# Weighted sums of the first attention stage, formed with the values as weights

## The chip, the cores and the metric

The kernel runs on one core of a Trainium2 chip. The metric is device time of one execution in microseconds (us). Before the change three runs gave 1503.12, 1503.74 and 1511.39 us; the median is 1503.74.

## What is computed

Two attentions one behind the other (32 packed queries `p` gather from keys and values, then the 576 queries gather from the packed result), then two gated MLPs. Cut from the reference:

```python
batch, n_heads, seq, head_dim, n_pack = 8, 8, 576, 64, 32
def sm_attn(qq, kk, vv):
    s = scale * np.matmul(qq, kk.transpose(0, 1, 3, 2))
    s = s - np.max(s, axis=-1, keepdims=True)
    a = np.exp(s)
    a = a / (np.sum(a, axis=-1, keepdims=True) + 1e-09)
    return np.matmul(a, vv)
p_packed = sm_attn(p, k, v)
out = sm_attn(q, p_packed, p_packed)
# x: out as (4608, 512)
h = x @ w_in;  y = (h * sigmoid(h)) @ w_out
h2 = y @ w_in2;  result = (h2 * cos(h2)) @ w_out2
```

## The kernel before

The program records every operation first and a planner then sets the order. `Plan.add` notes what each operation reads and writes and gives it a cost from a table (`price`, lines 163 to 193); `Plan.schedule` places the operations on the engines by these costs and by due times (`due_first`, line 1186); the instructions are then written out in that order, each engine's in its own queue. Buffers are rings: a ring's next tile is handed out in the order in which the program records, so an operation that writes it waits for the last reader of what it held. An operation recorded inside `plan.either()` may go to ScalarE or VectorE, as the planner finds. Where the planner sees TensorE idle in the first 60 us, it puts in filler matmuls (`busy`, line 1201; 64 columns, result unused). Since all operations are written out by one helper, the profile shows line 213 for nearly everything, and tiles tell them apart.

*First stage* (`stage1`, line 808), once for each batch b and group g of four heads. The keys come turned (`mem.turned`); `scores` multiplies them with the packed queries (tile `pbd`) into two banks of PSUM; the row maximum, the copy to `a1` and the exponential follow, which also sums each row (`sums`); `rs` is the reciprocal of the sum (lines 824 to 826). `a1` holds 128 rows (four heads of 32 packed queries) and 576 columns. It is turned in chunks by TensorE (line 835) and copied to `a1t`: five chunks of 128 columns, the last of 64, in the steady class `Steady`; six of 96 in `Boot`, which serves batches 0 and 1. Then come the weighted sums (lines 840 to 850): the softmax chunk is the weight (32 columns, one head), the values move (64 columns):

```python
for c in range(n):
    for j in range(2):
        for h2 in range(2):
            h = 32 * (2 * j + place(g, h2))
            T.matmul(st[h : h + 32, :D], a1t[: lens[c], c, h : h + 32], vt(c, h2, j), ...)
```

The result is scaled by `rs` into `pp` (line 852), turned once more by TensorE (line 854) and copied to `ppf` (line 856), which is what the second stage and `products` read. In the trace `a1`, `a1t` and `pp` are tiles `big` in the steady class, and `ba`, `bat` and `bpp` in the boot class; the values are `vin`, and `bx` in the boot class.

*Second stage* (`stage2`, line 860): scores of all queries against `ppf`, softmax on VectorE and ScalarE, and the turned result as a pair of rounded parts in `a2` (trace: `a`), a ring of six buffers, two for a batch. *Products* (line 907) multiply `ppf` with the first MLP's input weights, so that the first MLP (`first`, line 955) reads `a2` and these products. It runs in 208 steps of 16 hidden blocks: 64 steps for batches 0 and 1 (`BLOCKS[0]`), then nine blocks of 16 steps over 320 or 512 tokens. The attention of batches 2 to 7 is recorded between these steps by `firsts` (line 1221), `seconds` (line 1228) and the loops from line 1269 on. From about 700 us the second MLP runs.

Of the kernel before, what the change touches and what calls it, by code (L numbers as in the profile page):

```python
# [12 lines left out]
F32 = mybir.dt.float32  # L13
F32R = mybir.dt.float32r
I32 = mybir.dt.int32
U32 = mybir.dt.uint32
AF = mybir.ActivationFunctionType
ALU = mybir.AluOpType
# [417 lines left out]
def attention_mlps_kernel(  # L436
# [13 lines left out]
    B, H, S, D = q.shape  # L450
# [3 lines left out]
    P = 128  # L454
# [12 lines left out]
    plan = Plan(nc)  # L467
# [4 lines left out]
    V, A, T, G, DMA = plan.V, plan.A, plan.T, plan.G, plan.D  # L472
# [7 lines left out]
    def ring(ts):  # L480

        at = cycle(ts)
        return lambda: next(at)
# [5 lines left out]
    bpool = boot_stack.enter_context(pool("boot", "right"))  # L489
# [4 lines left out]
    a2p = mid.enter_context(pool("a2p"))  # L494
    top = mid.enter_context(ExitStack())
    att = top.enter_context(pool("att"))
# [3 lines left out]
    def tiles(pl, shape, dtype, name, n):  # L500

        ts = [pl.tile(shape, dtype, name=f"{name}{i}") for i in range(n)]
        cells.setdefault(pl, []).extend(t.tensor.name for t in ts)
        return ts


    def place(g, h2):
        return (g + h2) % 2
# [39 lines left out]
    ident = const.tile([P, P], F32, name="ident")  # L548
# [10 lines left out]
    def copy(dst, src):  # L559
        with plan.either():  # L560
            A.copy(dst, src)
            V.tensor_copy(dst, src)
# [93 lines left out]
    mx2s = ring(tiles(att, [P, NB], F32, "mxb", 2))  # L656
    rs2s = ring(tiles(att, [P, NB], F32, "rsb", 2))
    ppfs = ring(tiles(att, [P, 2, 2 * NP], F32, "ppf", 4))
    a2s = ring(tiles(a2p, [P, 2, S], F32R, "a2", 6))

    pin = {}

# [19 lines left out]
    def cut(t, shape):  # L682
        t = t[:, : math.prod(shape[1:])]
        return t if len(shape) == 2 else t.rearrange("p (a b) -> p a b", a=shape[1])
# [4 lines left out]
    class Steady:  # L689
# [4 lines left out]

        def __init__(self):
            self.kins = ring(tiles(att, [P, NB, 32], F32, "kin", 2))
            self.vins = ring(tiles(att, [P, 4 * len(self.chunks), D], F32, "vin", 1))
            self.bigs = ring(tiles(att, [P, len(self.chunks) * P], F32, "big", 3))

        def get(self, name, shape, g, j=0):  # L700
            return cut(self.bigs(), shape)

        def turned(self, src, b, g, bank):

# [35 lines left out]
    class Boot:  # L740
# [7 lines left out]
        def __init__(self):  # L748
            self.x = dict(zip("kvq", tiles(bpool, [P, H, NCH, D], F32, "bx", 3)))
            self.kt = tiles(bpool, [P, S], F32, "bkt", 4)  # L750
            self.a = tiles(bpool, [P, S], F32, "ba", 2)
            self.at = tiles(bpool, [P, NCH * P], F32, "bat", 2)
            self.pp = tiles(bpool, [P, P], F32, "bpp", 2)

        def load(self, n, src, b):
            plan.unit = ("load", n, b)
# [8 lines left out]
        def get(self, name, shape, g, j=0):  # L765
            if name == "a1":
                return self.a[g]
            return cut({"kt": self.kt[2 * g + j], "s": self.a[g], "pp": self.pp[g]}.get(name, self.at[g]), shape)

        def turned(self, src, b, g, bank):  # L770
            x = self.x["k" if src is k else "q"]
# [16 lines left out]
    ppf = {}  # L788
    a2 = {}
# [18 lines left out]
    def stage1(b, g, bank, mem):  # L808
        plan.unit = ("stage1", b, g)

        plan.margin = plan.SPARE if b >= 2 else 0
        chunks = mem.chunks
        kt = mem.turned(k, b, g, bank)
        a1 = mem.get("a1", [P, S], g)
        mx = maxes()
        sts = scores(g, pbds[b % 2][:, 2 * g : 2 * g + 2], lambda h2: h2, kt, bank, mem.spot)
        for hf, st in enumerate(sts):
            V.tensor_reduce(mx[:, hf : hf + 1], st, axis=AX.X, op=ALU.max)
            copy(a1[:, hf * HALF : (hf + 1) * HALF], st)
        m = ms()  # L820
        V.tensor_scalar(m, mx[:, 0:1], mx[:, 1:2], -SCALE, op0=ALU.max, op1=ALU.mult)
        sums = sumss()
        A.activation(a1[:, :S], a1[:, :S], AF.Exp, bias=m, scale=SCALE, accum_out=sums)
        rs = rss()
        V.tensor_scalar(rs, sums, 1e-9, None, op0=ALU.add)
        V.reciprocal(rs, rs)
        chunks = mem.chunks
        n = len(chunks)
        lens = [len(range(S)[c]) for c in chunks]
        a1t = mem.get("a1t", [P, n, P], g)  # L830
        for c0, c1 in ((0, 4), (4, n)):
            st = bank()
            r = lens[c0]
            for c in range(c0, c1):
                T.transpose(st[:r, (c - c0) * P : (c - c0 + 1) * P], a1[:, chunks[c]], ident)
            copy(a1t[:r, c0:c1, :], st[:r, : (c1 - c0) * P].rearrange("p (c n) -> p c n", n=P))
        vt = mem.values(b, g)
        st = bank()
        with plan.together():
            for c in range(n):  # L840
                for j in range(2):
                    for h2 in range(2):
                        h = 32 * (2 * j + place(g, h2))
                        T.matmul(
                            st[h : h + 32, :D],
                            a1t[: lens[c], c, h : h + 32],
                            vt(c, h2, j),
                            start=(c == 0),
                            stop=(c == n - 1),
                        )  # L850
        pp = mem.get("pp", [P, 2, D], g)
        V.tensor_scalar(pp, st[:, :D].unsqueeze(1).to_broadcast([P, 2, D]), rs, None, op0=ALU.mult)
        st = bank()
        T.transpose(st[:, :P], pp.rearrange("p h d -> p (h d)"), ident)
        t = ppfs()
        copy(t, st[:, :P].rearrange("p (j n) -> p j n", j=2))
        ppf[b, g] = t
        plan.margin = 0

    def stage2(b, g, bank, mem):  # L860
# [331 lines left out]
    boot = Boot()  # L1192
# [28 lines left out]
    def firsts(b, mem, banks):  # L1221
        if b % 2 == 0:
            load_p(b)
        place_p(b)
        for g in range(2):
            stage1(b, g, banks[g], mem)

    def seconds(b):
        for g in range(2):
            for f in stage2(b, g, bank, steady):  # L1230
                f()
# [7 lines left out]
    boot.load("q", q, 0)  # L1239
    pairs = [ring([acc[g], acc[2 + g]]) for g in range(2)]  # L1240
    for g in range(2):
        stage1(0, g, pairs[g], boot)
    fs = [stage2(0, g, ring([hb[g], pairs[g]()]), boot) for g in range(2)]
    for f in sum(map(list, zip(*fs)), []):
        f()
# [23 lines left out]
    for o in range(BLOCKS[0]):  # L1269
# [3 lines left out]
        x = o - 48  # L1273
        if x >= 0 and x % 4 == 3:
            products(x // 4, (2,))
    firsts(3, steady, [bank, bank])
    for j, s0 in enumerate(BLOCKS[:-1]):
        b = 3 if j == 0 else j // 3 * 2 + j % 3 + 3 if j % 3 else B
        if j == 6:
            plan.release = LATER  # L1280
            for F in range(2):
                for c in range(2):
                    win2_unit(F, c)
                for c in range(4 * F, 4 * F + 4):
                    wout2_unit(c)
                    wout2_unit(c + FH)
            plan.release = 0.0
        for o in range(FC):
            first(s0 + o)
            if b < B:  # L1290
                if o % 4 == 3:
                    products(o // 4, (b,))
                if o == 7:
                    seconds(b)
        if j % 3 < 2 and (n := j // 3 * 2 + j % 3 + 4) < B:
            firsts(n, steady, [bank, bank])

    change(top, [att], "yp", "right", raws + ys, {len(raws) + i: n for i, n in ((1, 32), (2, 32), (3, 32), (4, 32), (5, 64), (6, 64), (7, 64), (8, 64))})
    change(mid, [a2p], "cp", "left", ns + rs_ + g2s + os_)
# [44 lines left out]
```

## Time and profile before

| | us |
|---|---|
| three runs | 1503.12, 1503.74 (median), 1511.39 |
| the profiled execution, its own time | 1507.88 |
| its span, first to last instruction | 1506.1 |
| busy: TensorE | 1492.0 (99%) |
| busy: VectorE | 1147.5 (76%) |
| busy: ScalarE | 756.6 (50%) |
| granted TensorE clock, mean | 0.996 |

The trace belongs to the profiled execution, which took 1.8 us beyond its span. Busy time of TensorE (PE) counts matmuls from issue to modelled end, so neighbours overlap; the distance from one start to the next tells what a matmul costs. PEld is the loading of weights, which overlaps PE. The granted clock is 1.00 for 2.4 GHz and 0.50 for 1.2 GHz.

### The profile page before, as it was taken

The numbers are of one execution on the slowest core, as the hardware profiler recorded it, in microseconds if no ns is written. First come the engines' busy times: TensorE is split into PE (matmuls) and PEld (weight loads), VectorE is DVE, ScalarE is ACT, GpSimd is POOL, SyncE is SP. The second block draws the span as 40 slices with busy tenths as digits, with TensorE's granted clock in tenths as the row PEclk, the third lists the DMA queues.
The fourth block names the chain that finished last, engine by engine and source line by source line (L and its number), as shares of the span: only waits on it lengthen the run. The fifth ranks groups of instructions, "written<-read, shape, count | busy, mean of one in ns | idle before, by whom it ended". The sixth has DMA issues, their size and how long they took to land.

```text
span 1506.1 us, 29441 instructions
## 1 busy us (share of the span) xinstructions
PE 1492.0 (99%) x10790; PEld 1329.8 (88%) x10790; DVE 1147.5 (76%) x2361; ACT 756.6 (50%) x1554; POOL 0.7 (0%) x6
## 2 busy tenths in 40 slices
PE   8999999999999999999999999999999999999998
PEld 6898988878998888989989999899989999999997
DVE  6899877977787967866387778878777777777765
ACT  6776554645455454545454444544444444444443
POOL 0000000000000000000000000000000000000000
PEclk9899999999999999999999999999999999999999
DMA  9676666676767666465776658676666657575550
GB/s 266 197 229 192 171 179 158 166 199 164 201 175 232 165 189 174 144 224 180 263 259 205 203 180 268 203 248 215 218 198 200 203 181 227 177 229 179 186 190 33
DMA packets 313968, 296.23 MB, mean 197 GB/s; under 512 B 172512, under 2 KB 218080, under 8 KB 313824
## 3 DMA queue, kind: packets, MB, share of 16 engines
q1 hardware_dynamic: 313824, 294.35, 64.7%
q8 instruction: 85, 1.39, 0.4%
q14 instruction: 59, 0.48, 0.1%
HBM read 242.81 MB, written 51.45 MB: 195 GB/s over the span
## 4 chain that ended last, share of the span: by engine, by line
PE 92%; DMA 3%; DVE 2%; SPq 1%; ACT 1%; issue 0%; DVEq 0%; ACTq 0%
PE acc L213 51%; PE hb L213 23%; PE mb L213 9%; PE sb L213 9%; DMA ysb<-ypart 2%; SPq L213 1%; DVE r L213 1%; DMA wd<-in_moe_w_in 1%; PE acc L1203 0%; DMA w<-w2s 0%; DMA bx<-in_k 0%; DVE raw L213 0%; ACT bkt L213 0%; DVE wd L213 0%; DMA out<-o 0%
## 5 line engine op out<-in xcount | busy, mean ns | idle before, releaser
L213 PE MATMUL acc<-g,w 128*128 128x320 f32 (+2 forms) x2496 | 469.1, 327 | 0.0
L213 PE MATMUL acc<-w,g 128*128 128x512 f32 x1728 | 432.0, 392 | 0.1
L213 PEld LDWEIGHTS acc<-g,w 128*128 128x128 f32 x2496 | 383.8, 188 | 45.3 <-issue 23.4
L213 PEld LDWEIGHTS acc<-w,g 128*128 128x128 f32 x1728 | 310.6, 189 | 56.3 <-ACT ysb L213 0.5
L213 PE MATMUL hb<-a,w 128*128 128x320 f32 (+2 forms) x1536 | 264.7, 299 | 2.5 <-DVE gf L213 2.2
L213 PEld LDWEIGHTS hb<-a,w 128*128 128x128 f32 x1536 | 227.4, 190 | 22.4 <-issue 8.2
L213 DVE TENSOR_TENSOR g<-gf,g 128x320 fp32r<-128x320 f32 (+2 forms) x208 | 107.8, 521 | 53.5 <-PE acc L213 41.0
L213 ACT ACTIVATE gf<-hb 128x320 f32<-128x320 f32 (+2 forms) x208 | 95.4, 466 | 102.8 <-PE hb L213 89.8
L213 ACT CAST g<-gf 128x320 fp32r<-128x320 f32 (+2 forms) x186 | 90.9, 490 | 103.8 <-PE acc L213 88.0
L213 DVE SCALAR_TENSOR_TENSOR gf<-gf,hb 128x320 f32<-128x320 f32 (+2 forms) x208 | 105.1, 517 | 40.8 <-ACT gf L213 39.8
L213 ACT ACTIVATE r<-r,half_pi 128x512 f32<-128x512 f32 x144 | 103.6, 720 | 36.9 <-DVE r L213 36.6
L213 ACT CAST g<-r 128x512 fp32r<-128x512 f32 x144 | 89.5, 621 | 60.4 <-DVE r L213 58.0
L213 PEld LDWEIGHTS hb<-w,w 128*128 128x128 f32 x744 | 105.5, 190 | 8.0
L213 PE MATMUL hb<-w,w 128*128 128x256 f32 x744 | 111.8, 282 | 0.0
L213 DVE TENSOR_TENSOR g<-r,g 128x512 fp32r<-128x512 f32 x144 | 98.7, 686 | 11.9 <-ACT g L213 11.6
L213 DVE SCALAR_TENSOR_TENSOR r<-n,r 128x512 f32<-128x512 int32 x144 | 99.0, 687 | 2.3
L213 ACT ACTIVATE n<-hb 128x512 int32<-128x512 f32 x72 | 43.1, 598 | 109.7 <-PE hb L213 107.7
L213 DVE TENSOR_TENSOR hb<-hb,gf 128x256 f32<-128x256 f32 x72 | 31.1, 431 | 68.5 <-PE hb L213 68.2
L213 ACT ACTIVATE n<-mb 128x512 int32<-128x512 f32 x36 | 21.5, 598 | 95.0 <-PE mb L213 95.0
L213 PE MATMUL mb<-w,w 128*128 128x256 f32 x456 | 65.8, 283 | 0.0
L213 PE MATMUL sb<-w,w 128*128 128x256 f32 x456 | 65.8, 283 | 0.0
L213 DVE TENSOR_SCALAR r<-r 128x512 f32<-128x512 f32 x144 | 60.8, 423 | 2.6
(206 smaller groups left out, 1897.0 us busy)
## 6 DMA issues: line engine op xcount, KB each, us to landing
w<-w2s SPq DMA_DIRECT2D x504, 256.0 KB, 3.6
w<-w1dram SPq DMA_DIRECT2D x96, 256.0 KB, 4.0
w2s<-wd SPq DMA_DIRECT2D x28, 512.0 KB, 3.9
wd<-in_moe_w_in SPq DMA_DIRECT2D x24, 512.0 KB, 4.8
wd<-in_moe_w_out SPq DMA_DIRECT2D x20, 512.0 KB, 4.2
raw<-ydram SPq DMA_DIRECT2D x72, 128.0 KB, 3.8
w2dram<-wd SPq DMA_DIRECT2D x16, 512.0 KB, 2.9
w<-w2dram SPq DMA_DIRECT2D x16, 512.0 KB, 5.5
```

The source lines that it names most:

```text
L213: run = lambda: emit(*[real(x) for x in args], **{k: real(x) for k, x in kw.items()})
```

## The change

- `a1` is multiplied by `rs` right behind the exponential (576 columns, ScalarE or VectorE); the scaling into `pp` is gone.
- `stage1` ends with the turned chunks; a new function `weighted` forms the sums, for both groups of a batch in one piece and one bank (for batches 0 and 1 group by group). The values are the weights now (64 columns) and the softmax chunk moves (32 columns), so that the result comes out turned: the transpose of `pp` is gone. The chunks are the inner loop under j.
- `ppf` is filled by four copies of 64 rows by 64 elements for each group, where it was one of 128 by 128.
- Buffers: `a2` four in place of six; `vin` two in place of one; the turned chunks get two buffers `a1t` of their own, and the three `bigs` shrink to 576 columns.
- The loops: `firsts(3)` is recorded in step 59 in place of behind step 63; `seconds` always at a block's first step in place of its eighth, and for batches 4 to 7 one block later.

```diff
-    a2s = ring(tiles(a2p, [P, 2, S], F32R, "a2", 6))
+    a2s = ring(tiles(a2p, [P, 2, S], F32R, "a2", 4))
...
-            self.vins = ring(tiles(att, [P, 4 * len(self.chunks), D], F32, "vin", 1))
-            self.bigs = ring(tiles(att, [P, len(self.chunks) * P], F32, "big", 3))
+            self.vins = ring(tiles(att, [P, 4 * len(self.chunks), D], F32, "vin", 2))
+            self.bigs = ring(tiles(att, [P, S], F32, "big", 3))
+            self.a1ts = ring(tiles(att, [P, len(self.chunks) * P], F32, "a1t", 2))
...
-        chunks = mem.chunks
+        with plan.either():
+            V.tensor_scalar(a1[:, :S], a1[:, :S], rs, None, op0=ALU.mult)
+            A.activation(a1[:, :S], a1[:, :S], AF.Copy, scale=rs)
...
-        vt = mem.values(b, g)
+        plan.margin = 0
+        return lens, a1t, mem.values(b, g)
+
+    def weighted(b, parts, bank):
+        plan.unit = ("stage1", b, min(parts))
+
+        plan.margin = plan.SPARE if b >= 2 else 0
         st = bank()
         with plan.together():
-            for c in range(n):
+            for i, (g, (lens, a1t, vt)) in enumerate(parts.items()):
+                n = len(lens)
                 for j in range(2):
-                    for h2 in range(2):
-                        h = 32 * (2 * j + place(g, h2))
-                        T.matmul(
-                            st[h : h + 32, :D],
-                            a1t[: lens[c], c, h : h + 32],
-                            vt(c, h2, j),
-                            start=(c == 0),
-                            stop=(c == n - 1),
-                        )
-        pp = mem.get("pp", [P, 2, D], g)
-        V.tensor_scalar(pp, st[:, :D].unsqueeze(1).to_broadcast([P, 2, D]), rs, None, op0=ALU.mult)
-        st = bank()
-        T.transpose(st[:, :P], pp.rearrange("p h d -> p (h d)"), ident)
-        t = ppfs()
-        copy(t, st[:, :P].rearrange("p (j n) -> p j n", j=2))
-        ppf[b, g] = t
+                    for c in range(n):
+                        for h2 in range(2):
+                            h = 32 * (2 * j + place(g, h2))
+                            T.matmul(
+                                st[64 * h2 : 64 * h2 + 64, D * i + 32 * j : D * i + 32 * j + 32],
+                                vt(c, h2, j),
+                                a1t[: lens[c], c, h : h + 32],
+                                start=(c == 0),
+                                stop=(c == n - 1),
+                            )
+        for i, g in enumerate(parts):
+            t = ppfs()
+            for h2 in range(2):
+                for r in (64 * h2, 64 - 64 * h2):
+                    x = 32 * place(g, h2)
+                    copy(t[r : r + 64, :, x : x + 32], st[64 * h2 : 64 * h2 + 64, D * i : D * i + D].rearrange("p (j n) -> p j n", j=2))
+            ppf[b, g] = t
         plan.margin = 0
...
-        for g in range(2):
-            stage1(b, g, banks[g], mem)
+        parts = {g: stage1(b, g, banks[g], mem) for g in range(2)}
+        if b == 1:
+            for g in range(2):
+                weighted(b, {g: parts[g]}, banks[g])
+        else:
+            weighted(b, parts, banks[0])
...
-    firsts(3, steady, [bank, bank])
+        if o == 59:
+            firsts(3, steady, [bank, bank])
...
-        b = 3 if j == 0 else j // 3 * 2 + j % 3 + 3 if j % 3 else B
+        x = j // 3 * 2 + 2
+        b = (3 if j == 0 else B, x + 2, x + 3)[j % 3]
+        c = (x + 1, B, x + 2)[j % 3]
...
-            if b < B:
-                if o % 4 == 3:
-                    products(o // 4, (b,))
-                if o == 7:
-                    seconds(b)
+            if b < B and o % 4 == 3:
+                products(o // 4, (b,))
+            if c < B and o == 0:
+                seconds(c)
```

**How the order moves.** TensorE, the weighted sum of batch 2's second group, before the change (`acc` and `hb` are the first MLP, `vin` the moving values, `big` the softmax as weights; a call stands for two passes; first the moving operand, then the weights):

```order
L213 MATMUL acc_88<-g_154,w_1098 128x288
L213 MATMUL acc_89<-g_154,w_1098 128x288
L213 MATMUL sb<-vin_176,big_179 32x64 x20
L213 MATMUL acc_90<-g_154,w_1098 128x288
L213 MATMUL acc_91<-g_154,w_1098 128x288
L213 MATMUL hb_93<-a_136,w_1102 128x288 x3
```

and the sums of batch 2 with the change:

```order
L213 MATMUL acc_90<-g_152,w_1108 128x288
L213 MATMUL acc_91<-g_152,w_1108 128x288
L213 MATMUL sb<-a1t_177,vin_172 64x32 x20
L213 MATMUL sb<-a1t_178,vin_173 64x32 x20
L213 MATMUL acc_90<-g_152,w_1108 128x288
L213 MATMUL acc_91<-g_152,w_1108 128x288
L213 MATMUL hb_92<-a_136,w_1111 128x288 x3
```

Both groups stand together; the values have become the weights, the output is 64 rows by 32 columns, and there are 40 calls in one piece where there were 20 twice.

TensorE in the start, the sums of batch 0 (`bat` the softmax, `bx` the values, `bpp` the scaled result, line 1203 and after it line 1213 the fillers, `w1e,ppf` the first products), before:

```order
L213 MATMUL acc_88<-bx_158,bat_166 32x64 x24
L1203 MATMUL acc_89<-ident 128x64 x3
L213 MATMUL acc_90<-ident,bpp_168 128x128
L1203 MATMUL acc_88<-ident 128x64
L213 MATMUL mb<-w1e_146,ppf_132 32x512 x2
L213 MATMUL mb<-w1e_147,ppf_132 32x512 x2
L1203 MATMUL acc_88<-ident 128x64 x14
L213 MATMUL acc_89<-bx_158,bat_167 32x64 x24
```

and with the change:

```order
L213 MATMUL acc_88<-ident,ba_162 96x128 x4
L213 MATMUL acc_90<-ident,ba_162 96x128 x2
L1213 MATMUL acc_89<-ident 128x64 x9
L213 MATMUL acc_89<-ident,ba_163 96x128 x4
L213 MATMUL acc_91<-ident,ba_163 96x128 x2
L213 MATMUL acc_88<-bat_164,bx_156 64x32 x24
L1213 MATMUL acc_89<-ident 128x64 x3
L213 MATMUL mb<-w1e_144,ppf_132 32x512 x2
L213 MATMUL mb<-w1e_145,ppf_132 32x512 x2
L1213 MATMUL acc_88<-ident 128x64 x8
L213 MATMUL acc_89<-bat_165,bx_156 64x32 x24
```

The transpose of `bpp` is gone between sum and product; nine fillers stand ahead of the second group's transposes, and eight in place of fourteen ahead of its sum.

VectorE, the last writing of `a2` for batch 5 with the change (`a_139`; `gf<-gf,hb` is the multiplication of a step of the first MLP, of which 126 stand ahead of it):

```order
L213 SCALAR_TENSOR_TENSOR gf_148<-gf_148,hb_92 128x320
L213 STREAM_TRANSPOSE big_175<-big_174 128x576
L213 SCALAR_TENSOR_TENSOR gf_149<-gf_149,hb_93 128x320
L213 STREAM_TRANSPOSE big_174<-kin_171 128x576
L213 TENSOR_TENSOR a_139<-big_175,a_139 128x576
L213 TENSOR_TENSOR g_151<-gf_148,g_151 128x320
```

Before, the same writing went to a buffer of its own, `a_141`, behind 120 multiplications; it has come six steps nearer to step 128, which reads it.

## Rows read from the trace of the kernel before

**Rows 1.** The page, part 1 (busy us, share, instructions) and part 4 (chain by engine).

```profile
PE 1492.0 (99%) x10790; PEld 1329.8 (88%) x10790; DVE 1147.5 (76%) x2361; ACT 756.6 (50%) x1554; POOL 0.7 (0%) x6
PE 92%; DMA 3%; DVE 2%; SPq 1%; ACT 1%; issue 0%; DVEq 0%; ACTq 0%
```

**Rows 2.** Stretches of the span; the first line names the columns.

```profile
core 0: us, PE busy (x) PEld busy (x) DVE busy (x) ACT busy (x) POOL busy (x), PEclk, DMA share, GB/s
0.00:40.00 40.00, 34.11 (x433) 27.08 (x433) 26.18 (x79) 24.77 (x59) 0.70 (x6) 1.00 1.02 265
40.00:44.00 4.00, 3.83 (x31) 2.21 (x30) 3.56 (x11) 3.38 (x8) 0.00 (x0) 0.64 1.08 251
44.00:48.00 4.00, 4.00 (x19) 4.00 (x20) 3.58 (x9) 3.30 (x9) 0.00 (x0) 0.50 1.06 244
48.00:52.00 4.00, 4.00 (x21) 3.91 (x21) 0.99 (x6) 1.79 (x6) 0.00 (x0) 0.58 1.04 335
52.00:80.00 28.00, 27.14 (x275) 23.80 (x274) 27.43 (x76) 23.68 (x60) 0.00 (x0) 1.00 0.42 141
80.00:700.00 620.00, 618.54 (x4993) 543.47 (x4992) 487.99 (x985) 333.70 (x706) 0.00 (x0) 1.00 0.66 184
700.00:1506.00 806.00, 800.37 (x5030) 725.29 (x5028) 597.76 (x1204) 365.94 (x711) 0.00 (x0) 1.00 0.63 204
```

**Rows 3.** Order of time, TensorE, around batch 2's first weighted sum (start, us, what).

```profile
148.08 1.36 PE L213 MATMUL hb<-a,w 128*128 128x288 f32 x9
149.27 0.56 PE L213 MATMUL acc<-g,w 128*128 128x288 f32 x3
...
156.35 0.82 PE L213 MATMUL acc<-g,w 128*128 128x288 f32 x5
157.10 0.90 PE L213 MATMUL sb<-vin,big 128*32 128x64 f32 x40
157.93 0.40 PE L213 MATMUL acc<-g,w 128*128 128x288 f32 x1
158.17 0.82 PE L213 MATMUL hb<-a,w 128*128 128x288 f32 x5
```

**Rows 4.** Order of time, TensorE, around the transpose of that sum.

```profile
159.75 0.27 PE L213 MATMUL mb<-ident,big 128*128 128x128 f32 x1
159.78 0.51 PE L213 MATMUL hb<-a,w 128*128 128x288 f32 x2
160.12 0.29 PE L213 MATMUL acc<-g,w 128*128 128x288 f32 x1
```

**Rows 5.** Order of time, TensorE, batch 0's two weighted sums and the fillers between.

```profile
16.07 0.88 PE L213 MATMUL acc<-bx,bat 96*32 96x64 f32 x48
16.88 0.32 PE L1203 MATMUL acc<-ident 128*128 128x64 f32 x1
...
18.74 0.63 PE L213 MATMUL mb<-w1e,ppf 64*32 64x512 f32 x4 [0.18 <-ACT ppf L213]
...
19.73 3.34 PE L1203 MATMUL acc<-ident 128*128 128x64 f32 x28
23.00 0.88 PE L213 MATMUL acc<-bx,bat 96*32 96x64 f32 x48
23.80 0.30 PE L213 MATMUL hb<-ident,bx 96*128 96x96 f32 x1
...
25.46 0.63 PE L213 MATMUL sb<-w1e,ppf 64*32 64x512 f32 x4
```

**Rows 6.** Groups by line and form, 80 to 700 us (busy us, mean ns, idle before).

```profile
L213 ACT ACTIVATE big<-big 128x576 f32<-128x576 f32 x12 | 8.2, 686 | 5.2 <-DVE big L213 5.2
L213 DVE TENSOR_SCALAR big<-sb,rs 128x128 f32<-128x128 f32 x12 | 4.2, 348 | 2.7 <-PE sb L213 1.5 <-ACT g L213 1.2
L213 ACT COPY ppf<-mb 128x128 f32<-128x128 f32 x12 | 3.2, 263 | 5.5 <-PE mb L213 5.4
L213 DVE TENSOR_SCALAR rs<-sums 128x1 f32<-128x1 f32 x12 | 1.8, 150 | 3.3 <-ACT big L213 3.3
```

**Rows 7.** Order of time, TensorE's longest wait between 80 and 700 us.

```profile
584.58 0.41 PE L213 MATMUL hb<-a,w 128*128 128x320 f32 x1 [1.46 <-DVE gf L213]
```

More of the change, by code (lines that the diff above doesn't have):

```diff
@@ L696, in __init__ @@
             self.kins = ring(tiles(att, [P, NB, 32], F32, "kin", 2))
-            self.vins = ring(tiles(att, [P, 4 * len(self.chunks), D], F32, "vin", 1))
-            self.bigs = ring(tiles(att, [P, len(self.chunks) * P], F32, "big", 3))
+            self.vins = ring(tiles(att, [P, 4 * len(self.chunks), D], F32, "vin", 2))
+            self.bigs = ring(tiles(att, [P, S], F32, "big", 3))
+            self.a1ts = ring(tiles(att, [P, len(self.chunks) * P], F32, "a1t", 2))
         def get(self, name, shape, g, j=0):
-            return cut(self.bigs(), shape)
+            return cut((self.a1ts if name == "a1t" else self.bigs)(), shape)
         def turned(self, src, b, g, bank):
@@ L752, in __init__ @@
             self.at = tiles(bpool, [P, NCH * P], F32, "bat", 2)
-            self.pp = tiles(bpool, [P, P], F32, "bpp", 2)
         def load(self, n, src, b):
@@ L767, in get @@
                 return self.a[g]
-            return cut({"kt": self.kt[2 * g + j], "s": self.a[g], "pp": self.pp[g]}.get(name, self.at[g]), shape)
+            return cut({"kt": self.kt[2 * g + j], "s": self.a[g]}.get(name, self.at[g]), shape)
         def turned(self, src, b, g, bank):
@@ L1241, in attention_mlps_kernel @@
     for g in range(2):
-        stage1(0, g, pairs[g], boot)
+        weighted(0, {g: stage1(0, g, pairs[g], boot)}, pairs[g])
     fs = [stage2(0, g, ring([hb[g], pairs[g]()]), boot) for g in range(2)]
@@ L1289, in attention_mlps_kernel @@
             first(s0 + o)
-            if b < B:
-                if o % 4 == 3:
-                    products(o // 4, (b,))
-                if o == 7:
-                    seconds(b)
-        if j % 3 < 2 and (n := j // 3 * 2 + j % 3 + 4) < B:
-            firsts(n, steady, [bank, bank])
+            if b < B and o % 4 == 3:
+                products(o // 4, (b,))
+            if c < B and o == 0:
+                seconds(c)
+        if j % 3 < 2 and x + 2 + j % 3 < B:
+            firsts(x + 2 + j % 3, steady, [bank, bank])
     change(top, [att], "yp", "right", raws + ys, {len(raws) + i: n for i, n in ((1, 32), (2, 32), (3, 32), (4, 32), (5, 64), (6, 64), (7, 64), (8, 64))})
```

## The prediction

> **What bounds the kernel now.** I read the head of the page and its chain first: TensorE is busy 1492.0 of 1506.1 us and makes up 92% of the chain [rows 1]. Then the stretches [rows 2]. From 80 to 700 us, where the first MLP runs and the attention of batches 2 to 7 is slipped in between its matmuls, TensorE is busy 618.54 of 620 us at the full granted clock; VectorE has 488 and ScalarE 334 of the 620. So in that stretch each nanosecond of work that TensorE gains or loses moves the end, and work on the other two is hidden while it comes in time. Up to 80 us it is different: TensorE also runs filler matmuls and waits, VectorE is busy 27.43 of 28 us from 52 to 80, and between 40 and 52 the granted clock falls, to 0.50 (1.2 of 2.4 GHz) in 44 to 48. From 700 us on nothing is changed. The question is therefore what the new weighted sums cost TensorE. For that I read its order of time around one weighted sum, one transpose, and the start [rows 3 to 5].
>
> **The old weighted sum, taken apart.** Each call is two passes (20 calls, 40 instructions). Four tiles of 32 output rows work side by side, so four instructions make a round. In the start, 48 instructions are 12 rounds in one tile shape and one change of shape at the end: 16.07 to 16.88 us, 0.81 [rows 5]. In a later batch, 40 instructions are 10 rounds, with a change at the last chunk (64 rows in place of 128) and one at the end: 157.10 to 157.93, 0.83 [rows 3]. From 12r + s = 0.81 and 10r + 2s = 0.83 come r = 0.056 and s = 0.13 us. Around it: matmuls of 288 columns stand 0.132 apart (nine in 1.19 us). The five ahead of the sum should have ended at 157.01, so the entry cost 0.09; the one behind it took 0.24, 0.11 too much [rows 3]. One sum of one group costs 0.83 + 0.20 = 1.03 us. The transpose of its result: from 159.75 to 160.12 stand it and two matmuls of 0.132, so it costs 0.106 [rows 4]. A batch (two groups) costs 2 x 1.03 + 2 x 0.106 = 2.27 us.
>
> **The new one.** The values are now the weights (64 columns) and the turned softmax moves (32 columns). There are as many instructions, 80 for a batch, but only two tiles of 64 output rows side by side: 40 rounds in place of 20. What is a round? The fillers have 128-column weights and move the same 64 columns as the old sums; they stand 3.27/28 = 0.117 us apart [rows 5], twice the 0.056 of the 32-column tiles. With the same moving columns only the weights differ, so I read their loading as the pace there: 0.117 for 128 columns, 0.058 for 64. The lower bound is that only the moving columns count: half of 0.056, 0.028. I take 0.056, being nearest to the filler row, which alone shows wide weights.
>
> What the Trainium skill says here, in TensorEngine Tiling (Array Packing), Theoretical Speedup, speaks against the gain and against my pace as well: a dimension up to 32 gives a factor of 4, up to 64 of 2. Half the tiles with half the columns would then be even, the lower bound; the filler row speaks against it. By that rule the later batches' term below is -0.9 us, by the rows +5.8.
>
> The loop now takes the two pairs of heads (j) outside and the chunks inside. Thus each of the four (group, j) parts of a batch ends in the 64-row chunk and changes shape twice: 8 changes, where before there were 4. A change waits for the last pass to run out, and that pass is half as long now, so s lies between 0.13 and 0.13 - 0.028 = 0.10; I take 0.10. A batch has one entry and exit, 0.20, since both groups stand in one piece. Sum: 40 x 0.056 + 8 x 0.10 + 0.20 = 3.24 us, against 2.27: **+0.97 a batch, +5.8 us for batches 2 to 7**. With s = 0.13 it is +7.3; with rounds of 0.028 it is 1.12 + 0.80 + 0.20 = 2.12, or -0.9 in all.
>
> **The start (batches 0 and 1).** Four groups of 12 rounds become 24: +0.67 us each, 2.7 on TensorE; four transposes go (about 0.4), and batch 1's groups stand together (-0.2). Fillers go from 53 to 57 in the program, 0.23 each, mostly in time that is idle anyway. On the path of group 0: the normalising comes ahead of the transposes, two small operations of about 0.15 [rows 6] and a pass over 576 columns, bounded by 0.69 on ScalarE [rows 6], with hand-overs about +0.9; the sum +0.67; behind it went 1.86 us from the end of the sum (16.88) to the first product (18.74), by way of scale, transpose and copy [rows 5], and four copies, at most 0.26 each [rows 6], take about 1.3 of these back. Net +1.0. Group 1's sum begins at 23.00 behind fillers; its normalising is hidden there, and the 1.66 us to 25.46 [rows 5] lose 0.4 and gain 0.67: +0.3. These overlap with loads and VectorE's queue, so I take **+1.0 us** for the whole start, between -2 (all of the shorter tail counts and the longer sums lie in idle time) and +4.
>
> **Off the path.** Per group VectorE loses a scaling of 0.35 us and the normalising pass goes to either engine, at most 0.69; three more copies at most 0.79 [rows 6]. Over 12 groups that is at most 18 us more for ScalarE, which has 286 idle of the 620 [rows 2]: nothing. If that cover fails, TensorE waits on ScalarE's casts behind a string of seven copies, at most 1.8 us each time. Loads are as many as before; the second buffer for values only lets them start earlier. Stage 1 of batch 3 is recorded some steps earlier, and stage 2 of batches 4 to 7 a block later, with all its transposes and loads; TensorE's work in it is the same. Four turned-softmax buffers in place of six mean that batch b can only be written once b-2 has been read. Its last write stands, on VectorE, behind 76, 108, 126, 156 and 175 first-MLP multiplications for batches 3 to 7, and is needed at steps 80, 112, 128, 160, 176; before it was 80, 94, 120, 144, 174. The one large wait there, 1.46 us at 584.58, was for a multiplication [rows 7]. I put nothing.
>
> **Sum.** +5.8 + 1.0 = +6.8 us. The profiled execution took 1507.88 us, 1.8 outside its span, so its like would take 1514.7. It lies 4.1 above the median of 1503.74; from the median: **1510.5 us**, +0.45%. Half a per cent, 7.5 us, is about what a measurement of this kernel tells from no change, so the forecast is a small loss just inside that.
>
> **Rivals.**
> - *Streaming is the pace* (0.17). Rounds of 0.028 give -0.9 in the batches, and the start +0.3: about 1503. For it: tiles of 32 columns show no cost of weights at all. Against it: the filler row.
> - *Buffers come late* (0.12; slower). With four buffers a write waits for the last step that reads the old batch, and TensorE stands at the block's start. One such stop costs what the late multiplication cost, 1.46 us [rows 7]. It decides when VectorE's write comes later than the step that needs it, which batch 7 (one step ahead) and batch 5 (two) are nearest to; three stops make 1515. Against it: batch 3 was written with no step to spare before, and no wait is seen there.
> - *The half clock goes* (0.10). The granted clock was 0.64, 0.50 and 0.58 in three stretches of 4 us [rows 2], 4 x (0.36 + 0.50 + 0.42) = 5.1 us of lost work. TensorE works more in the start now (longer sums, four more fillers); if the drop does not come: 1505.4.
> - *It comes twice* (0.08): +5.1, 1515.6. TensorE ahead of the drop was busy 34.11 of 40 us [rows 2], and small shifts decide.
> - Forecast as it stands: 0.53. That the change does not do what it says is excluded by the order: the weights and the moving operand are exchanged in all 16 groups, and the 16 transposes are gone.
>
> **How the numbers follow.** Slower by over 0.5% (above 1511.3): of the forecast's 0.53 some 0.22, since its upper bound for the change of shape alone passes it; late buffers 0.12; two drops 0.07: 0.41. Faster by over 0.5% (below 1496.2) needs streaming, no drop and a shorter start together: 0.05. Within: 0.54. Range: the forecast with its bounds reaches from 1505 (start at -2, part of the rounds hidden) to 1514; streaming reaches down to 1502, a second drop or late buffers up to 1518. I give 1502 to 1518.
>
> **What will show it.** One sum of a batch should be one piece of 80 matmuls lasting about 3.0 us to the next full-width matmul, against 0.83 twice; about 1.9 if streaming is the pace. From 80 to 700 us there should be the same work ending 6 us later with TensorE still without idle. Wrong would be: weight loads of 64 columns no longer than those of 32 in their spacing; new waits of TensorE on VectorE or ScalarE at a block's start; a start longer or shorter by more than 4 us.

## The result and the profile after

Eleven runs of the changed kernel have a median of 1515.11 us (1512.59 to 1519.82), against 1503.53 (1501.04 to 1512.06) for the kernel before beside them: a ratio of 1.0066, 95% interval 1.0047 to 1.0085, or +11.6 us. The forecast was 1510.5 with a range of 1502 to 1518. The time lies in the range, but the loss is 1.7 times the 6.8 us that were summed, and on the other side of the half per cent.

The profiled execution took 1513.29 us with a span of 1511.3. The head and the chain of its page answer to [rows 1]:

```profile
PE 1497.4 (99%) x10782; PEld 1336.6 (88%) x10782; DVE 1138.5 (75%) x2341; ACT 776.7 (51%) x1622; POOL 0.7 (0%) x6
...
PE 95%; ACT 2%; DMA 2%; DVE 1%; issue 0%; SPq 0%; ACTq 0%; DVEq 0%
```

TensorE is busy 5.4 us longer, and its share of the chain rises. The stretches, in the columns of [rows 2]:

```profile
0.00:40.00 40.00, 33.27 (x376) 26.16 (x376) 24.18 (x69) 25.40 (x64) 0.70 (x6) 1.00 1.01 271
40.00:44.00 4.00, 3.34 (x35) 2.23 (x35) 4.00 (x14) 4.00 (x12) 0.00 (x0) 1.00 1.06 256
44.00:48.00 4.00, 3.14 (x25) 2.86 (x24) 3.73 (x12) 4.00 (x12) 0.00 (x0) 1.00 1.06 256
48.00:52.00 4.00, 4.00 (x70) 3.78 (x71) 4.00 (x10) 3.27 (x8) 0.00 (x0) 1.00 1.05 297
52.00:80.00 28.00, 27.59 (x279) 24.55 (x276) 26.05 (x70) 23.93 (x63) 0.00 (x0) 1.00 0.50 159
80.00:700.00 620.00, 620.00 (x4952) 546.60 (x4951) 473.15 (x958) 345.13 (x750) 0.00 (x0) 1.00 0.65 180
700.00:1511.00 811.00, 806.02 (x5060) 730.43 (x5059) 603.35 (x1214) 370.94 (x721) 0.00 (x0) 1.00 0.64 205
```

Three things are to be seen. From 80 to 700 us TensorE is busy all 620 us, where it was 618.54. The granted clock is 1.00 in every stretch: the drop to 0.50 that stands in [rows 2] did not come in this execution. And between 40 and 48 us VectorE and ScalarE are full (15.7 of 16 us together), while TensorE has 1.5 of 8 us idle.

One later batch, in order of time on TensorE; it answers to the sum in [rows 3]:

```profile
161.56 0.68 PE L213 MATMUL acc<-g,w 128*128 128x288 f32 x4
162.18 3.36 PE L213 MATMUL sb<-a1t,vin 128*64 128x32 f32 x80
165.47 0.53 PE L213 MATMUL acc<-g,w 128*128 128x288 f32 x2
165.84 0.69 PE L213 MATMUL hb<-a,w 128*128 128x288 f32 x4
```

The piece of 80 lasts 165.47 - 162.18 = 3.29 us to the next full-width matmul, and the entry and exit are those of before: four matmuls at 0.132 from 161.56 end at 162.09, 0.09 ahead of it, and the two behind take 0.37 in place of 0.26.

Batch 0's sums in the start, which answer to [rows 5], and what ScalarE does just ahead of them:

```profile
14.90 2.12 PE L1213 MATMUL acc<-ident 128*128 128x64 f32 x18
17.67 0.86 PE L213 MATMUL acc<-ident,ba 128*96 128x128 f32 x6 [0.65 <-ACT ba L213]
18.46 1.59 PE L213 MATMUL acc<-bat,bx 96*64 96x32 f32 x48
19.98 0.88 PE L1213 MATMUL acc<-ident 128*128 128x64 f32 x6
20.80 1.07 PE L213 MATMUL mb<-w1e,ppf 64*32 64x512 f32 x8
21.79 2.00 PE L1213 MATMUL acc<-ident 128*128 128x64 f32 x16
23.72 1.59 PE L213 MATMUL acc<-bat,bx 96*64 96x32 f32 x48
```

```profile
16.25 0.71 ACT L213 ACTIVATE wde<-wde 128x512 int32<-128x512 uint32 x1
16.84 0.78 ACT L213 ACTIVATE ba<-ba,rs 128x576 f32<-128x576 f32 x1
```

TensorE waits 0.65 us for the normalising of group 1 (16.84 on ScalarE, behind the making of weights), whose transposes stand in its queue ahead of group 0's sum. That sum begins at 18.46, where it was 16.07, and lasts 1.52 in place of 0.81; the first product is at 20.80, where it was 18.74.

**Where the time lies.** Two marks cut the run: the 201st matmul of `acc<-g,w` (at 100.79 us before, 101.15 after, counted in the trace) and the first matmul of the second MLP. The latter, before and then after:

```profile
728.42 0.28 PE L213 MATMUL mb<-y,w 128*128 128x256 f32 x1
```

```profile
734.40 0.28 PE L213 MATMUL mb<-y,w 128*128 128x256 f32 x1
```

Between the marks the run grew from 627.63 to 633.25, +5.6 us. Up to the first mark it grew by only 0.4, but the execution before had lost 5.1 us there to its half clock (as the prediction worked out), so at equal clock the start is 5.5 us longer. Behind the second mark the span is 0.8 shorter. Together that is 10.3 us. The medians, 11.6 apart, also hold what the half clock cost in either set of runs.

What the middle consists of, from the starts of TensorE's matmuls between the marks: the weighted sums of six batches take 19.76 us, where they took 9.96 (+9.8). Six entries and exits fewer are worth -1.2. The wait of 1.46 [rows 7] is gone, and no wait of TensorE is listed in that stretch any more. The transposes of `big` went from 60 to 48 matmuls but from 4.81 only to 4.66 us in their own spacing. These make 7.0; the other -1.4 lies in the spacing of the first MLP's matmuls, where the exits of the lost transposes lie too, and is not told apart.

### The profile page after: what moved, and what is told of

It reads as the page before. It is cut to its first block, busy times and chain, and to the rows that moved or that the text cites. A ratio compares the mean times of both kernels' runs of the same rounds, so it can differ in the third digit from the quotient of the medians.

```text
span 1511.3 us, 29451 instructions
## 1 busy us (share of the span) xinstructions
PE 1497.4 (99%) x10782; PEld 1336.6 (88%) x10782; DVE 1138.5 (75%) x2341; ACT 776.7 (51%) x1622; POOL 0.7 (0%) x6
## 3 DMA queue, kind: packets, MB, share of 16 engines
q8 instruction: 85, 1.39, 0.4%
## 4 chain that ended last, share of the span: by engine, by line
PE 95%; ACT 2%; DMA 2%; DVE 1%; issue 0%; SPq 0%; ACTq 0%; DVEq 0%
PE acc L213 53%; PE hb L213 23%; PE mb L213 10%; PE sb L213 9%; DMA ysb<-ypart 1%; DVE r L213 1%; ACT ba L213 0%; DMA w<-w2s 0%; ACT bkt L213 0%; ACT wde L213 0%; DMA bx<-in_k 0%; PE acc L1213 0%; ACT wy L213 0%; DVE w L213 0%; DVE o L213 0%
## 5 line engine op out<-in xcount | busy, mean ns | idle before, releaser
L213 PE MATMUL hb<-a,w 128*128 128x320 f32 (+2 forms) x1536 | 259.8, 297 | 1.4 <-DVE gf L213 0.7
L213 DVE TENSOR_TENSOR g<-r,g 128x512 fp32r<-128x512 f32 x144 | 98.8, 687 | 12.3 <-ACT g L213 12.1
```

The lines of the kernel that those rows point to most:

```text
L213: run = lambda: emit(*[real(x) for x in args], **{k: real(x) for k, x in kw.items()})
```

## The experiments

All times are medians beside the runs of the kernel before on the same chip (1505.26, 1505.00 and 1504.13 us in the three sets, 28, 19 and 23 runs), and each edit is against the changed kernel.

**e5_old_all, e4_old_start, e3_old_later: which part costs what.** The old `weighted` (values moving, scaling into `pp`, transpose) is put back everywhere, in batches 0 and 1, or in batches 2 to 7; buffers, loops and order rules stay as changed.

```diff
+    def old_way(b):
+        return True      # e4: b < 2    e3: b >= 2
...
+        if old_way(b):
+            for g in range(2):
+                weighted_old(b, g, stage1(b, g, banks[g], mem), banks[g], mem)
+            return
```

> Old weighted sums everywhere (scaled behind, transposed), with the new buffers and the new recording order. Theory 1 (the loss lies in the sums: +7.3 us in batches 2 to 7, the rest in the start): as the kernel before, 1503.5 us within 2. Rival (four buffers for the turned softmax and the later second stages cost): 1507 or more, with waits of TensorE on VectorE between 200 and 700 us.

> New sums in batches 2 to 7 alone, old ones in batches 0 and 1. Theory 1: 1503.5 + 7.3 = 1510.8 us, six pieces of 80 matmuls of 3.29 us each. Rival (most of the loss is in the start): 1507 or less. Rival (order and buffers): 1514 or more.

> New sums in batches 0 and 1 alone, old ones in batches 2 to 7. Theory 1: the start costs what is left, about 4.3 us: 1507.8. Rival (the start costs the 1.0 us of the prediction): 1504.5.

| new sums in | us | ratio, 95% interval | against before | median of the runs at 0.999 or 1.000 |
|---|---|---|---|---|
| none (e5) | 1507.18 | 1.0016 (1.0006 to 1.0026) | +1.9 | 1507.17 |
| batches 2 to 7 (e4) | 1509.09 | 1.0025 (1.0012 to 1.0039) | +3.8 | 1508.63 |
| batches 0 and 1 (e3) | 1512.92 | 1.0046 (1.0028 to 1.0064) | +7.7 | 1511.56 |
| all (after) | 1515.11 | 1.0066 (1.0047 to 1.0085) | +11.6 | 1513.24 |

By the medians the start is the larger part: e3 less e5 is 5.7, after less e4 is 7.8. The later batches cost 1.9 (e4 less e5) to 3.9 (after less e3), though each piece is 3.29 us long in e4 as well. New buffers and order alone cost 1.9.

But the runs that are compared differ in their granted clock: of the 28 runs of the kernel before in this set 11 list a mean of 0.998 or less, of e5's 12 only one. The last column leaves such runs out; for the kernel before it would be 1503.82. The differences are then 3.4 for buffers and order, 1.5 to 1.7 for the later batches and 4.4 to 4.6 for the start, which add up to the whole of 9.4 (the changed kernel's runs are from another set than the other three).

The marks agree. In e5, whose profiled execution had no half clock, the first mark is at 95.90 us, where the kernel before would have it without its 5.1 of lost clock (95.7). The middle takes 631.06 us, 3.4 more than 627.63. So more than half of the 5.6 by which the middle grew comes with buffers and order, and against e5 the new sums add 2.2. In e3, with the old sums there, the middle is 633.49 us, no shorter than with the new ones. These are single executions.

TensorE's waits from 80 to 700 us in e5 (what waited for what: us in total, times, longest):

```profile
PE acc L213 <- DVE g L213: 1.9, 2, 1.1
```

The kernel before has one wait of 1.46 there [rows 7], so waits make 0.4 of the 3.4; the rest is not told apart. In e4 the same list is empty and TensorE is busy 620.00 us. Why the waits go is not shown. More work on TensorE alone does not explain it, for the list of e2 below is empty too, and its sums take hardly more than the old ones (2.23 + 0.20 a batch against 2.27).

**e1_chunks_outside: the changes of shape.** The chunks become the outermost loop, so that a batch has two changes of shape where it had eight.

```diff
-            for i, (g, (lens, a1t, vt)) in enumerate(parts.items()):
-                n = len(lens)
-                for j in range(2):
-                    for c in range(n):
+            n = len(next(iter(parts.values()))[0])
+            for c in range(n):
+                for i, (g, (lens, a1t, vt)) in enumerate(parts.items()):
+                    for j in range(2):
...
-                                start=(c == 0),
+                                start=(c == 0 and i == j == 0),
```

> The changed kernel with the chunks as the outermost loop of a piece, over both groups and both pairs, so that the tile shape changes twice in a piece in place of eight times. If each change costs its 0.13 to 0.15 us: a piece of 80 takes 3.29 - 0.85 = 2.45 us, and the time falls by 5 us to 1510. If the changes of shape are hidden and the weights alone set the time: 3.29 and 1515.

1510.34 us, ratio 1.0044 (1.0024 to 1.0063), +5.1. TensorE around batch 2's piece:

```profile
166.76 2.64 PE L213 MATMUL sb<-a1t,vin 128*64 128x32 f32 x80
169.33 0.53 PE L213 MATMUL acc<-g,w 128*128 128x288 f32 x2
```

The piece is 2.57 us long, 0.72 less than 3.29 for six changes fewer: 0.12 for a change. The time is close to what was expected. The changed kernel's own rows give the same: the 48 instructions in the start, 24r + s = 1.52, and the piece, 40r + 8s = 3.29, make a round r = 0.058 and a change s = 0.12 us. So s is hardly shorter than the old 0.13, although the pass in front of it is half as long.

**e11_new_later_outside: the same in batches 2 to 7, with the old start.** e4's rule with e1's loop.

> Old sums in batches 0 and 1; new ones in batches 2 to 7 with the chunks outermost over both groups (a piece of 2.57 us in place of 3.29). The kernel with new sums in batches 2 to 7 alone stood 3.8 us above the kernel before. If work on TensorE is what counts: 6 x 0.72 = 4.3 us less, 0.5 below the kernel before. If waits come back in the place of the work: as before or above by up to 2 us.

1504.74 us, ratio 1.0001 (0.9987 to 1.0015), +0.6: 3.2 less than e4, where 6 x 0.72 = 4.3 was expected. With few changes the new form in the later batches, buffers and order included, costs about nothing against the kernel before.

**e2_narrow: is the loading of weights the pace?** Only 32 of the 64 value columns are weights; passes, chunks and moving columns are as changed. The kernel leaves out half of the first stage's output columns.

```diff
-                                st[64 * h2 : 64 * h2 + 64, D * i + 32 * j : D * i + 32 * j + 32],
-                                vt(c, h2, j),
+                                st[64 * h2 : 64 * h2 + 32, D * i + 32 * j : D * i + 32 * j + 32],
+                                vt(c, h2, j)[:, :32],
```

> The changed kernel with half of each value tile left out as weights: 32 weight columns in place of 64, in as many instructions and as many tiles side by side (half of the output columns of the first stage are not formed). The moving columns stay 32. If the loading of the weights sets the pace of a tile: rounds of 0.028 to 0.03 us in place of 0.056, a piece of 80 takes 3.29 - 1.06 = about 2.2 us, and batches 2 to 7 win 6 us, the start some of 2.6: 1507 to 1509. If a pass has a least time whatever its columns: rounds of 0.056, 3.2 us, 1515.

1505.22 us, ratio 1.0003 (0.9993 to 1.0014), +0.2:

```profile
163.98 2.30 PE L213 MATMUL sb<-a1t,vin 128*32 128x32 f32 x80
166.21 0.53 PE L213 MATMUL acc<-g,w 128*128 128x288 f32 x2
```

The piece is 2.23 us, and 48 instructions in the start take 0.88 in place of 1.52. Neighbouring rounds stand 0.032 us apart where they stood 0.058. The same number of passes moves the same columns, so the weights set the pace. Of the 11.4 us that e2 gives back, 6 x 1.06 = 6.4 are in the later pieces, and the middle is shorter by just that (626.86 us). That leaves 5.0 for the start, where the sums lost only 2.5 of work: 2 x 0.64 in batch 0 and 1.23 in batch 1. The first mark agrees: 102.95 us, of which 6.8 are lost clock, so 96.1 against 101.15.

**e8_start_plain, e7_start_vector: the normalising in the start.** It is left out in batches 0 and 1, or put on VectorE alone.

```diff
-        with plan.either():
-            V.tensor_scalar(a1[:, :S], a1[:, :S], rs, None, op0=ALU.mult)
-            A.activation(a1[:, :S], a1[:, :S], AF.Copy, scale=rs)
+        if b >= 2:       # e7: else V.tensor_scalar alone
+            with plan.either():
+                V.tensor_scalar(a1[:, :S], a1[:, :S], rs, None, op0=ALU.mult)
+                A.activation(a1[:, :S], a1[:, :S], AF.Copy, scale=rs)
```

> The changed kernel with the normalising left out in batches 0 and 1 (their sums are not divided). What is left of the loss in the start is then due to the longer sums and the copies. If the normalising ahead of the transposes makes the loss in the start: first product near 18.7 us and 3 us less, 1512. If the longer sums make it: 1514 to 1515.

> The changed kernel with the normalising of batches 0 and 1 on VectorE alone. In the changed kernel TensorE waited for ScalarE's normalising of group 1 ahead of the transposes behind which the sum of group 0 stands. If that wait makes the loss in the start: the first product comes at about 19.5 us in place of 20.8, and the time falls by 1 to 2 us, to 1513.5. If the longer sums and the place ahead of the transposes make it: 1515.

e8: 1511.88 us, ratio 1.0048 (1.0034 to 1.0062), +6.9. e7: 1513.56, ratio 1.0054 (1.004 to 1.0068), +8.6. By the medians the loss shrinks by 4.7 us without the pass. The ranges of the runs overlap (e8's is 1511.66 to 1513.52), and by the runs at 0.999 or 1.000 alone e8 stands at 1511.74, 1.5 below the changed kernel. The first marks, with no half clock ahead of either, are at 98.60 and 101.15 us, 2.6 apart. But the first product did not come at 18.7, as expected; it came at 22.63:

```profile
15.79 4.58 PE L1214 MATMUL hb<-ident 128*128 128x64 f32 x40
20.30 1.59 PE L213 MATMUL acc<-bat,bx 96*64 96x32 f32 x48
22.63 1.07 PE L213 MATMUL mb<-w1e,ppf 64*32 64x512 f32 x8
```

The planner filled the gap with 40 filler instructions, and the sum stood behind them. The gain lies later: batch 1's first product is at 52.11 us, against 56.17 in the changed kernel. In e7 the first product is at 20.35 us where 19.5 was expected. Its median is 3.0 below the changed kernel's, but here too the ranges of runs overlap, so nothing more is taken from it.

That the pass is on the path there can be read from the chain of the changed kernel from 37.92 us on (start, us, what):

```profile
37.92 0.78 ACT ba L213
38.69 0.58 ACT wde L213
39.27 0.32 ACT ba L213
39.60 0.47 ACT bat L213
40.07 0.34 ACT ba L213
40.41 0.26 ACT bat L213
40.67 0.58 ACT wy L213
```

The chain runs through ScalarE without a gap here: normalising, weights, parts of `ba` and `bat`. TensorE meanwhile is busy 17.86 of 20 us from 36 to 56:

```profile
36.00:56.00 20.00, 17.86 (x214) 15.61 (x214) 18.12 (x50) 17.64 (x47) 0.00 (x0) 1.00 1.00 269
```

Where batch 1 lost shows beside e5. Its second group in the changed kernel (`ba` the transposes, then both groups' sums, the last copy into `ppf`, the first product), and then in e5:

```profile
48.97 0.63 PE L213 MATMUL sb<-ident,ba 128*96 128x128 f32 x4
...
50.54 1.59 PE L213 MATMUL sb<-bat,bx 96*64 96x32 f32 x48
...
53.46 1.58 PE L213 MATMUL acc<-g,w 128*128 128x288 f32 x10
...
55.91 0.21 ACT L213 COPY ppf<-mb 64x64 f32<-64x64 f32 x1
56.17 0.63 PE L213 MATMUL mb<-w1e,ppf 64*32 64x512 f32 x4
```

```profile
45.59 0.60 PE L213 MATMUL sb<-ident,ba 128*96 128x128 f32 x4
...
47.52 0.88 PE L213 MATMUL sb<-bx,bat 96*32 96x64 f32 x48
48.33 0.93 PE L213 MATMUL acc<-g,w 128*128 128x288 f32 x5
...
49.96 0.63 PE L213 MATMUL mb<-w1e,ppf 64*32 64x512 f32 x4
```

The exponential of that group starts at 45.76 and 44.50 us, so the changed kernel is 1.3 behind there. From it to the transposes pass 3.21 and 1.09 us; the normalising stands between. From the start of the sums to the first product pass 5.63 and 2.44: the sums take 2.92 in place of 0.81, and behind them go 2.71 us in place of 1.63, until the last of eight copies into `ppf`, which stand between other work of ScalarE and VectorE. In e8, without the normalising, this last stretch is as long (46.36 to 52.11). Batch 1's first product is 6.2 us later than e5's; batch 0's is only 0.7 later (20.80 against 20.07).

**e9_group_by_group: batch 1's sums apart.** The sum of each group stands right behind its stage 1 instead of both behind both.

```diff
-        parts = {g: stage1(b, g, banks[g], mem) for g in range(2)}
-        if b == 1:
-            for g in range(2):
-                weighted(b, {g: parts[g]}, banks[g])
-        else:
+        if b == 1:
+            for g in range(2):
+                weighted(b, {g: stage1(b, g, banks[g], mem)}, banks[g])
+        else:
+            parts = {g: stage1(b, g, banks[g], mem) for g in range(2)}
             weighted(b, parts, banks[0])
```

> The changed kernel, but in batch 1 each group's sum is recorded right behind its stage 1, as in batch 0 (in the changed kernel both stage 1s come first, and TensorE formed both sums in one piece of 2.9 us at 50.5 us, where before group 0's stood at 37 us). If this is where the start loses: batch 1's first product comes at 52 us in place of 56, and the time falls by 3 to 4 us against the changed kernel. If the normalising on a full ScalarE makes it: at most 1 us.

1516.21 us, ratio 1.0068 (1.0048 to 1.0088), +12.1: no gain. The first group's sum moved from 50.54 to 40.00 us, but the products, which need both groups, came at 57.28, later than the 56.17 of the changed kernel:

```profile
40.00 1.59 PE L213 MATMUL sb<-bat,bx 96*64 96x32 f32 x48
...
53.84 1.59 PE L213 MATMUL mb<-bat,bx 96*64 96x32 f32 x48
...
57.28 0.63 PE L213 MATMUL mb<-w1e,ppf 64*32 64x512 f32 x4
```

The theory that batch 1's two sums stand too late because they are recorded together fell.

**e6_old_joined, e10_joined_start_apart: the joining, with the old operands.** Both groups' old sums of a batch form one piece with the chunks outermost (batches 2 to 7); in e6 batches 0 and 1 also do both groups' stage 1 ahead of the sums, in e10 they do not.

```diff
+            for c in range(n):
+                for g, (lens, a1t, vt, rs) in parts.items():
+                    for j in range(2):
+                        for h2 in range(2):
+                            h = 32 * (2 * j + place(g, h2))
+                            T.matmul(st[h : h + 32, D * g : D * g + D],
+                                     a1t[: lens[c], c, h : h + 32], vt(c, h2, j),
+                                     start=(c == 0 and g == 0), ...)
```

> Old sums (32 weight columns, 64 moving) everywhere, but in batches 2 to 7 for both groups of a batch in one piece with the chunks outermost: 20 rounds, two changes of shape and one entry in place of 20 rounds, four changes and two entries. Theory: a piece of 80 takes 20 x 0.056 + 2 x 0.13 = 1.38 us in place of 2 x 0.83, and an entry of 0.20 less, 0.48 us a batch, 2.9 us in all against the kernel with old sums and the new order: 1504.3. If the changes of shape hide: no difference to that kernel, 1507.

> Old sums everywhere; in batches 2 to 7 both groups in one piece with the chunks outermost (1.39 us in place of 2 x 0.83); batches 0 and 1 group by group as in the kernel with old sums and the new order, which it differs from in that one thing alone. That kernel stood 1.9 us above the kernel before. Theory: 6 x 0.47 = 2.8 us less, 0.9 below the kernel before. If the joined pieces also take waits away, as the measured 5 us below the kernel before suggest: 5 us or more below it.

e6: 1500.05 us, ratio 0.9967 (0.9953 to 0.9981), -5.0. e10: 1501.45, ratio 0.9973 (0.9958 to 0.9988), -2.7. Both beat the kernel before. TensorE in e6:

```profile
162.38 1.46 PE L213 MATMUL sb<-vin,a1t 128*32 128x64 f32 x80
163.77 1.31 PE L213 MATMUL acc<-g,w 128*128 128x288 f32 x8
```

One piece of 1.39 us stands for two of 0.83 [rows 3]. With one entry and exit less, that is 0.47 a batch, 2.8 us for six. e10 gained 4.6 on e5; the rest is not accounted for, nor is the further 2.3 of e6, whose interval overlaps e10's. The joined sums with the buffers and loops of the kernel before were not tried.

## Why the prediction was right and wrong

**The pace of the new sums** was right. Rounds of 64 weight columns stand 0.058 us apart where 0.056 was taken, and e2 shows that it is the weights. The rival that the moving columns are the pace (rounds of 0.028) falls with it. The exchange cost 9.8 us of TensorE's time in six batches. The rule of the Trainium skill that was set against the rows (TensorEngine Tiling (Array Packing), Theoretical Speedup) would have made it even, and e2's trace disagrees: 0.032 us against 0.058 for the same moving columns.

**The changes of shape** were a little too cheap: 0.10 was taken as s, since the last pass is half as long. The piece measured 3.29 us where 40 x 0.056 + 8 x 0.10 = 3.04 was expected: with s at 0.12, 0.16 of the difference is the changes and 0.10 the rounds. So the later batches' term, by the pieces, was +7.3 in place of +5.8. The stage ended 5.6 later. That this is so near the 5.8 is luck: a wait of 1.46 [rows 7] went that nobody had counted on, and beside e5 only 2.2 of the 5.6 belong to the new sums and 3.4 to buffers and order.

**The start** is the step that failed: "+1.0 us for the whole start, between -2 and +4". By the marks it is 5.5, by e3 less e5 5.7, or 4.4 by the runs at 0.999 or 1.000 alone: beyond the upper end each time. Three statements in it were wrong. The first is that Group 1's normalising "is hidden there". It stands on ScalarE at 16.84, TensorE waits for it, and group 0's sum is queued behind the transposes that wait: the path went through the other group, which was costed as off it. Beside e5, whose first product is at 20.07 without any normalising, this cost at most 0.7. The second is that batch 1 was counted as TensorE work alone, and there most of the loss lies. From 36 to 56 us its normalising passes stand on ScalarE (0.78 us each), the first of them in a chain that runs through ScalarE. The third is that the four copies take less than the old way by scale and transpose. They do in batch 0 (0.82 us from the sum to the product, 1.86 before), but in batch 1 it is 2.71 against 1.63 in e5. "Off the path" was worked out from 80 to 700 us alone, where ScalarE has 286 us idle; from 36 to 56 it has 2.4 of 20, and 2.2 in e5 without the pass: there was no cover. The sums' 2.7 us, of which "idle time" was to hide a part, were not hidden either: shortened by 2.5 they give back 5.0 (e2). Leaving the normalising out gives back 2.6 by the first mark (e8). Together that is more than the start lost, so the two overlap, and no run parts them cleanly. No run has the old copies with the new sums.

**Buffers and order** were put at nothing. No wait of TensorE for a buffer is listed in the changed kernel, so the stops that the rival of late buffers named did not come. But e5 shows +1.9 for order and buffers alone, and 3.4 by the runs at 0.999 or 1.000 and by its middle between the marks. Its two waits on VectorE's `g`, which do not occur in the changed kernel, explain 0.4 of that beside the 1.46 of before; the cause of the rest stays open, and no run parts buffers from order.

**The half clock.** The rival "the half clock goes" happened in the profiled execution, "it comes twice" did not; whether the change has to do with it is open (below).

**The side of the half per cent.** Slower had 0.41 and within had 0.54. With the start at 5.5 the forecast's own sum would have been 5.8 + 5.5 = 11.3.

## What to carry to other kernels

When operands of a tiled f32 matmul are exchanged, cost the round by the larger of weight columns and moving columns and then count how many tiles stand side by side: here both forms have 64, but the new one has half the tiles, so its rounds are twice as many. Count the changes of tile shape too (0.12 to 0.13 us each here) and put loops so that they are few; joining the old sums gained, where no form of the exchange did. And work out "hidden" anew for each stretch: a pass that has 286 us of cover in one stage may have none in the first 60 us, where its engine makes weights, and in an engine's queue the wait of one group delays the other. Before differences below 1% are added up, compare the mean clock of the runs: here it turned 1.9 us into 3.4.

## What the runs showed of the hardware

- **Round and size.** A round is one pass in each tile that stands side by side. Four f32 forms: 32 weight columns with 64 moving 0.056 us, 64 with 32 0.058, 32 with 32 0.032, 128 with 64 0.117 [rows 5]. All are 0.88 to 0.99 ns times the larger of the two.
- **A change of shape hardly shortens with the pass.** It costs 0.13 us with 64 moving columns and 0.12 with 32. The Trainium skill (TensorEngine Tiling (Array Packing), Key Properties) says that a switch of tiling mode needs the array to drain. The traces agree that there is a gap, and its 0.12 to 0.13 us hardly follow the length of the last pass.
- **The half clock comes and goes.** The same kernel has it in some executions and not in others. Of the 70 runs of the kernel before in the three sets, 20 list a mean granted clock of 0.998 or less. Of the changed kernel's 11, five do, with 0.992 at 1519.82 us and 1.000 at 1512.59. In e1's profiled execution it held for some 17 us:

```profile
32.00:36.00 4.00, 3.55 (x40) 2.66 (x37) 3.87 (x15) 2.77 (x8) 0.00 (x0) 1.00 1.06 264
36.00:40.00 4.00, 3.88 (x18) 3.67 (x19) 3.90 (x12) 2.92 (x7) 0.00 (x0) 0.61 1.08 246
40.00:44.00 4.00, 3.88 (x22) 3.28 (x20) 3.22 (x12) 3.28 (x8) 0.00 (x0) 0.50 1.05 250
...
48.00:52.00 4.00, 4.00 (x19) 4.00 (x19) 4.00 (x12) 3.07 (x8) 0.00 (x0) 0.50 1.05 235
52.00:56.00 4.00, 4.00 (x49) 3.76 (x49) 1.56 (x5) 1.78 (x5) 0.00 (x0) 0.76 0.79 277
```

TensorE was busy 3.55 of 4 us ahead of it there, and 3.34 and 3.14 of 4 in the changed kernel's profile, where no drop came. By the runs at 0.999 or 1.000 alone the changed kernel's median is 1513.24 us, and that of before 1503.6 to 1504.6, so some 2 to 3 us of the 11.6 may be a matter of how often the drop came in eleven runs. Whether the change makes it more frequent is open.
